# A gated linear attention with a maxout feed-forward block: the step list of the beginning in another order

## The chip, the cores and the metric

The kernel runs on one core of one Trainium2 chip. The metric is the device time of one execution in microseconds (us); a profile of one further execution shows the engines: TensorE (PE, matrix products), VectorE (DVE), ScalarE (ACT), GpSimd (POOL) and SyncE (SP, which here only issues transfers).

## The reference, cut to what matters

```python
# q, k, v, a_re, a_im: (4, 8, 768, 48); complex gates a, at most 0.999 in magnitude
a = a * min(|a|, 0.999) / (|a| + 1e-6)
for t in range(S):
    S_re, S_im = a_re*S_re - a_im*S_im + k[t] v[t]^T, a_re*S_im + a_im*S_re
    y[t] = q[t] @ S_re
x = y as (3072 tokens, 384)
h = max(x @ w1, x @ w2, x @ w3)        # w: (384, 768), float64 in memory
out = h @ w_out                        # (768, 384)
```

All inputs but the weights are float32. The recurrence is over 768 time steps for each of 4 x 8 heads.

## The kernel before, in words

**Tiles.** Time is cut into tiles of 128 steps, two halves of 64 each, for all 8 heads of one batch entry. Two batch entries, `x` and `y`, are worked side by side as a group; there are 12 groups (`NG`), six for each pair of entries. The recurrence inside a tile is turned into matrix products: the gates' logarithms and angles are summed along time, and queries and keys are scaled by exponentials and turned by sines before they are multiplied. The state is carried from tile to tile.

**Steps.** Every operation has a short name and a group number, such as `ukx:2` (step `uk`, batch entry x, group 2). `run` (line 747) maps a name to the function that issues its instructions. The names that matter here:

- `Lr`, `Li`, `Lq`, `Lk`, `Lv`: loads of the gates' real and imaginary part (one transfer of 192 KB), of q, k, v (four of 48 KB each), all from SP's queue.
- gates (line 372), on ACT and VectorE, for both entries at once or, in group 0, for one half (`0` or `1` at the end): `sqr`, `sqi`, `add`, `lnL`, `expe`, `expw`, `lne`, `relu`, `Lnop`, `abs`, `pw` (TensorE), `lnw`, `expL`, `mulw`, `mulai`, `stt`, `sign`, `cpai`, `cpar`, `atan`, `carry`, `mulr`, `addi`. Their results are a logarithm `Ln` and an angle.
- angles (452): `cs` sums the angle on TensorE, `t` and `nf` take off whole turns (ACT, VectorE), `af`, `sa`, `sb` make cosine and sine on ACT; `Cd` passes the last row to the next group by a transfer.
- turns (492): `sums`, `F` on TensorE sum the logarithm; `En`, `Ek`, `Eq`, `f0` to `f3` are exponentials on ACT; `mk`, `mq`, `uk`, `uq`, `kEn` scale and turn keys and queries on VectorE; `tpk`, `tpq` transpose them on TensorE; `Kc`, `Qc` copy them out on ACT.
- factors, scores, state, outputs (557 to 705): `Q1`, `Q2`, `Q3`, `QB`, `KB`, `QG` (VectorE); `A`, `B`, `dk`, `y` (TensorE); `g0` to `g3` and `h0` to `h3` (nearly all VectorE), `b0`, `b1` (ACT); `x` copies the tile's result, the feed-forward block's input, out of PSUM on ACT.
- up (712): `U` and two digits is an up product on TensorE (third of the hidden width, weight matrix), the same with a small `u` copies or takes the maximum (ACT for matrix 0, VectorE else). In group 0 there is one for each entry (`U20x`); later groups do both entries in one product of 256 columns. project (729): `O`, `o`, `D` are the down product, its copy and its store; in the list of the beginning `PO`, `Po`, `PD`.
- weights (301 to 346): they lie in memory as float64 and are turned into float32 on the chip, in twelve blocks: `WL` and a number is a block's load (768 KB), `Wa`, `Wd` are its steps on ACT, `Wb`, `Wc`, `We`, `Wf` on VectorE. A block's raw data lies in room that is later needed for something else, so a load can have to wait for the `Wf` of an earlier block.
- `Zf`, `Zv`, `Zg` clear buffers on VectorE; `CL` builds masks on GpSimd.

**What sets the order.** Nothing is left to a scheduler. `SCHEDULE` (line 21) lists the steps of the beginning, `CYCLE` (line 52) those of one group in the steady part, which `program` (787) runs for each group from 2 on. Each engine is wrapped in `Bound` (line 122), which makes every instruction follow the one before it on its engine, in the list's order; so SP, ACT, VectorE, TensorE and GpSimd are five queues, each in list order, that wait for one another only for data and buffers. All instructions are recorded through one line of that wrapper, 131, which is why the profile names this line throughout: steps are told apart by their tiles. TensorE's results go to four PSUM buffers in turn (`psum`, line 117): a product can start once the steps that read the fourth product before it are done. `activation` (150) loads another function table on ACT when the list goes from exponentials and logarithms to sines and arc tangents or back.

```python
def program(text, g):
    for word in text.split():
        name, at = word.split(":")
        run(name, g + int(at))
```

Of the kernel before, what the change touches and what calls it, by code (L numbers as in the profile page):

```python
# [56 lines left out]
cpai:1 g2x:0 QGx:0 cpar:1 Ox:-2 g3x:0 b0x:0 b1x:0 carry:1 mkx:1 KBy:0 U11:-1 mulr:1 addi:1 yx:0 xx:0 
u11:-1 kEny:0 ox:-2 U02:-1 csx:1 tx:1 csy:1 Q2y:0 ty:1 u02:-1 dky:0 sumsy:1 Lqx:1 nfx:1 sqi:2 mqx:1 afx:1
sbx:1 sax:1 nfy:1 h1y:0 Q1y:0 Eky:1 Q3y:0 Eny:1 h2y:0 Dy:-2 Fx:1 f0x:1 U12:-1 h3y:0 Eqy:1 uqx:1 u12:-1 Ay:0
add:2 f3x:1 g0y:0 g1y:0 By:0 g2y:0 f1x:1 f2x:1 lnL:2 g3y:0 QGy:0 expw:2 tpqx:1 expe:2 b0y:0 b1y:0 Oy:-1 ukx:1  # L60
relu:2 yy:0 tpkx:1 Qcx:1 xy:0
# [775 lines left out]
```

## Time and profile before

| | before |
|---|---|
| median of three runs | 626.19 us |
| the three runs | 624.35, 626.19, 628.63 us |
| the profiled execution's own time | 624.75 us |
| its span, first to last instruction | 622.9 us |
| TensorE, VectorE, ScalarE busy | 583.8, 478.9, 437.3 us |
| mean granted TensorE clock | 0.978 |

The span is cut into slices and stages below. Times of instructions are from the start of the span. "Busy" of TensorE is the time with a product under way, whether at full or at half clock; the granted clock is a share of full speed. A wait is idle time of an engine before an instruction, put down to the engine or transfer that ended it.

### The profile page before, as it was taken

What the parts mean: (1) busy time and instruction counts of PE and PEld (TensorE: products, weight loads), DVE (VectorE), ACT (ScalarE), POOL (GpSimd) and SP (SyncE); (2) the same over time, 40 slices, a digit from 0 to 9 for tenths busy, and PEclk for the clock granted to TensorE, in tenths of its full rate; (3) what the DMA queues carried; (4) which work ended last, traced back from release to release, by engine and by line L of the source; (5) the groups of instructions that cost most, each with busy time, mean ns of one, the idle gap of its engine ahead of it and who ended that gap; (6) DMA issues with size and microseconds to landing.
All of it is one profiled execution on the core that took longest, in us unless ns stands there. A gap on an engine that the chain in (4) does not pass through costs nothing.

```text
span 622.9 us, 22703 instructions
## 1 busy us (share of the span) xinstructions
PE 583.8 (94%) x10124; PEld 467.9 (75%) x10124; DVE 478.9 (77%) x694; ACT 437.3 (70%) x746; POOL 14.1 (2%) x47
## 2 busy tenths in 40 slices
PE   4376899999999999999999999999999999999997
PEld 1255787687887887887787788788788788788785
DVE  6998999989887887877777787887887887754211
ACT  8998998795894894894894994894894894641100
POOL 3500000000000000000000000000000000000000
PEclk9667999999999999999999999999999999999999
DMA  9787411442232223122222222222230221000000
GB/s 239 171 212 183 128 37 23 100 81 45 45 63 53 45 62 63 34 63 52 45 63 53 51 56 53 50 56 53 51 69 15 40 53 27 15 3 15 15 13 25
DMA packets 136544, 39.24 MB, mean 63 GB/s; under 512 B 129152, under 2 KB 132224, under 8 KB 136448
## 3 DMA queue, kind: packets, MB, share of 16 engines
q1 hardware_dynamic: 136448, 37.80, 27.5%
q8 instruction: 79, 1.29, 0.9%
q14 instruction: 17, 0.14, 0.1%
HBM read 33.03 MB, written 4.72 MB: 61 GB/s over the span
## 4 chain that ended last, share of the span: by engine, by line
PE 84%; ACT 7%; SPq 4%; DVE 3%; issue 1%; DMA 0%; DVEq 0%; ACTq 0%
PE up L131 44%; PE op L131 15%; PE y L131 6%; SPq L131 4%; PE A L131 4%; PE tp L131 4%; PE dk L131 3%; PE cs L131 2%; PE sums L131 2%; PE F L131 1%; ACT L131 1%; PE B L131 1%; DVE Q L131 1%; ACT L L131 1%; PE pw L131 1%
## 5 line engine op out<-in xcount | busy, mean ns | idle before, releaser
L131 PE MATMUL up<-xT,w 128*128 128x256 f32 (+1 forms) x1404 | 297.4, 368 | 2.4 <-ACT E L131 0.6
L131 PEld LDWEIGHTS up<-xT,w 128*128 128x128 f32 x1404 | 248.3, 191 | 40.1 <-ACT L L131 1.7
L131 DVE TENSOR_TENSOR hT<-hT,up 128x768 f32<-128x768 f32 (+1 forms) x56 | 46.8, 838 | 78.1 <-PE up L131 78.1
L131 PE MATMUL op<-wo,hT 128*128 128x384 f32 x288 | 98.8, 494 | 0.0
L131 DVE TENSOR_TENSOR Q<-Q,f 112x512 f32<-112x512 f32 (+2 forms) x72 | 68.6, 954 | 12.6 <-ACT Q L131 12.2
L131 PEld LDWEIGHTS op<-wo,hT 128*128 128x128 f32 x288 | 53.0, 190 | 33.4
L131 ACT ACT_TABLE_LOAD x47 | 60.3, 1283 | 1.6 <-PEq L821 0.8
L131 ACT COPY xT<-y 128x384 f32<-128x384 f32 x24 | 11.5, 479 | 51.6 <-PE y L131 51.6
L131 PE MATMUL y<-atm,vb 128*32 128x64 f32 x1152 | 39.4, 222 | 4.3 <-issue 3.0
L131 PEld LDWEIGHTS y<-atm,vb 128*32 128x32 f32 x1152 | 32.3, 110 | 14.2 <-issue 11.4
L131 ACT ACTIVATE f<-F 48x280 f32<-48x280 f32 x96 | 38.3, 399 | 2.5 <-PE F L131 1.2
L131 ACT ACTIVATE t<-cs 128x384 f32<-128x384 f32 x24 | 11.8, 492 | 39.0 <-PE cs L131 39.0
L131 PE MATMUL y<-QG,g 112*32 112x64 f32 x1408 | 38.4, 220 | 0.2 <-DVE QG L131 0.2
L131 ACT COPY atm<-B 32x128 f32<-32x128 f32 x96 | 24.4, 254 | 19.9 <-DVE atm L131 18.7
L131 PE MATMUL A<-Q,K 112*32 112x80 f32 x1536 | 32.9, 239 | 3.2 <-DVE Q L131 3.0
L131 PEld LDWEIGHTS y<-QG,g 112*32 112x32 f32 x1408 | 34.8, 110 | 0.5 <-DVE QG L131 0.3
L131 PEld LDWEIGHTS A<-Q,K 112*32 112x32 f32 x1536 | 28.1, 112 | 8.1 <-issue 3.1
L131 ACT COPY Q<-tp 112x1024 f32<-112x1024 f32 x24 | 24.3, 1013 | 12.2 <-PE tp L131 11.9
L131 DVE COPY_PREDICATED atm<-masko,A 128x256 f32<-128x256 uint8 x72 | 31.3, 435 | 1.4
L131 DVE TENSOR_TENSOR g<-g,dk 112x384 f32<-112x384 f32 x40 | 22.0, 550 | 9.7 <-PE dk L131 9.4
L131 PEld LDWEIGHTS dk<-vb,uk 64*48 64x48 f32 (+1 forms) x1408 | 23.5, 130 | 7.9 <-ACT K L131 2.7
L131 ACT COPY ot<-op 128x384 f32<-128x384 f32 x24 | 11.5, 478 | 25.5 <-PE op L131 25.4
(106 smaller groups left out, 887.9 us busy)
## 6 DMA issues: line engine op xcount, KB each, us to landing
ar<-in_a_re_dram SPq DMA_DIRECT2D x24, 192.0 KB
ai<-in_a_im_dram SPq DMA_DIRECT2D x24, 192.0 KB
q<-in_q_dram SPq DMA_DIRECT2D x96, 48.0 KB
k<-in_k_dram SPq DMA_DIRECT2D x96, 48.0 KB
vb<-in_v_dram SPq DMA_DIRECT2D x96, 48.0 KB
out_dram<-ot SPq DMA_DIRECT2D x24, 192.0 KB
raw<-in_moe_w_dram SPq DMA_DIRECT2D x5, 768.0 KB
w<-in_moe_w_dram SPq DMA_DIRECT2D x2, 768.0 KB
```

Source lines behind the costliest of these rows:

```text
L131: ins = f(*a, **kw)
```

## The change

Only the two lists at the top of the file differ. `CYCLE` holds the same steps in the same order and is only wrapped anew. `SCHEDULE` holds the same 467 steps in another order. GpSimd's instructions keep their order; on SP, ACT, VectorE and TensorE they are permuted. Among other moves: `Zg` stands ahead of `add0`; `sumsx:0` ahead of `pw0:0`; both key loads ahead of two weight blocks; `say:0` ahead of `b1x:0` and `b0x:0`; `tpky:0` ahead of `tpqy:0`, and both ahead of the first up product, which is now `U20x` and no longer `U00x`; `xx:0` behind `cpar:1`; the list ends on the same transposes. Cut to the stretches in question:

```diff
-Zf:0 Lrx:0 sqr0:0 Zv:0 Lix:0 sqi0:0 Liy:0 sqi1:0 add0:0 lnL0:0 expe0:0 expw0:0 Lry:0 sqr1:0 lne0:0 WL0:0
-relu0:0 Lnop0:0 Wa0:0 abs0:0 pw0:0 Wd0:0 add1:0 lnL1:0 Wb0:0 Wc0:0 We0:0 Wf0:0 WL1:0 Wa1:0 Wb1:0 Liy:1 Lry:1
-expe1:0 expw1:0 Zg:0 WL7:0 lne1:0 relu1:0 Lnop1:0 Lqy:0 Wd1:0 sumsx:0 lnw0:0 Wc1:0 We1:0 Wf1:0 abs1:0 Wa7:0
-Wb7:0 Wc7:0 pw1:0 Enx:0 Eqx:0 Lkx:0 expL0:0 mulw0:0 mulai0:0 stt0:0 lnw1:0 sign0:0 expL1:0 mulai1:0 mulw1:0
-Wd7:0 We7:0 Wf7:0 cpai0:0 Ekx:0 mkx:0 cpar0:0 CL:0 stt1:0 atan0:0 mulr0:0 csx:0 WL3:0 Wa3:0 Fx:0 Wb3:0 Wc3:0
-WL2:0 Lrx:1 Wa2:0 Wb2:0 Wc2:0 Wd2:0 We2:0 Wf2:0 sign1:0 sqr:1 Lix:1 Lqx:0 atan1:0 cpai1:0 Lky:0 tx:0 nfx:0
-cpar1:0 mulr1:0 Wd3:0 We3:0 Wf3:0 afx:0 Lvx:0 sbx:0 mqx:0 WL8:0 csy:0 Liy:2 sqi:1 Lry:2 WL6:0 Cdx:0 sax:0
-ukx:0 tpkx:0 uqx:0 tpqx:0 kEnx:0 f3x:0 add:1 f1x:0 f0x:0 f2x:0 ty:0 nfy:0 Qcx:0 Q1x:0 lnL:1 Q2x:0 dkx:0 WL4:0
...
-Wc6:0 abs:1 sumsy:0 Eny:0 g0x:0 Lky:1 We6:0 g1x:0 Fy:0 f3y:0 f2y:0 Eqy:0 mqy:0 f0y:0 Wa8:0 Wf6:0 g2x:0 Wb8:0
-Wd8:0 g3x:0 pw:1 lnw:1 Wc8:0 We8:0 Bx:0 f1y:0 Cdy:0 Eky:0 mky:0 WL5:0 Lrx:2 afy:0 WL9:0 expL:1 mulai:1 mulw:1
-stt:1 b1x:0 b0x:0 yx:0 sby:0 Lix:2 say:0 Lvy:1 uqy:0 tpqy:0 Lqx:1 uky:0 Lkx:1 sign:1 Wf8:0 WL10:0 xx:0 Lvx:2
-Lqy:1 U00x:0 cpai:1 carry:1 atan:1 cpar:1 mulr:1 tpky:0 kEny:0 Wa4:0 Wb4:0 Qcy:0 Q2y:0 QBy:0 Q1y:0 Wa5:0 Wb5:0
-csx:1 tx:1 nfx:1 Cdx:1 sqr:2 u00x:0 U01x:0 Kcy:0 KBy:0 Q3y:0 sqi:2 add:2 sbx:1 Wc4:0 u01x:0 afx:1 sax:1 Wc5:0
-sumsx:1 Ekx:1 Enx:1 csy:1 ty:1 Liy:3 Lix:3 Ay:0 g0y:0 QGy:0 Wd4:0 We4:0 Eqx:1 mqx:1 g1y:0 nfy:1 Cdy:1 lnL:2
-expe:2 expw:2 relu:2 lne:2 U02x:0 g2y:0 u02x:0 g3y:0 Wf4:0 Wa9:0 WL11:0 mkx:1 Lnop:2 Wb9:0 uqx:1 U10x:0 u10x:0
-U21x:0 Wd5:0 U20x:0 u20x:0 u21x:0 By:0 b0y:0 abs:2 We5:0 dky:0 h1y:0 Wc9:0 Fx:1 f3x:1 f1x:1 addw:2 h2y:0 Lvx:1
...
-f3y:1 Ax:1 g0x:1 f1y:1 kEnx:1 POx:0 Pox:0 Lrx:3 Lry:3 QBx:1 g1x:1 KBx:1 g2x:1 mqy:1 g3x:1 Bx:1 b0x:1 uqy:1
-Lqx:2 QGx:1 sqi:3 mky:1 h0x:1 uky:1 dkx:1 h1x:1 b1x:1 tpqy:1 Qcy:1 Q2y:1 h2x:1 POy:0 yx:1 sqr:3 add:3 Lkx:2
-Q1y:1 lnL:3 Poy:0 xx:1 h3x:1 tpky:1 Kcy:1 Fx:2 f1x:2 f0x:2 f3x:2 f2x:2 csy:2 ty:2 Q3y:1 Ay:1 h0y:1 sumsx:2
-Ekx:2 Enx:2 QBy:1 kEny:1 KBy:1 By:1 g0y:1 Eqx:2 nfy:2 sumsy:2 Eny:2 g1y:1 PDy:0 g2y:1 g3y:1 b0y:1 dky:1 b1y:1
-expe:3 mqx:2 uqx:2 tpqx:2 Qcx:2 expw:3 QGy:1 h1y:1 mkx:2 Eqy:2 Eky:2 yy:1 xy:1 relu:3 PDx:0 h2y:1 ukx:2 tpkx:2
-h3y:1
...
+Zf:0 Lix:0 Zv:0 Zg:0 sqi0:0 Lrx:0 sqr0:0 add0:0 Liy:0 sqi1:0 Lry:0 WL0:0 WL1:0 Lky:0 WL3:0 WL7:0 lnL0:0
+expe0:0 expw0:0 lne0:0 Lkx:0 relu0:0 Lnop0:0 sumsx:0 sqr1:0 add1:0 Wa0:0 Wb0:0 Wc0:0 abs0:0 pw0:0 lnL1:0 Wd0:0
+We0:0 Wf0:0 Wa1:0 Wb1:0 Wc1:0 expe1:0 expw1:0 lne1:0 relu1:0 Lnop1:0 Wd1:0 We1:0 Wf1:0 lnw0:0 abs1:0 Eqx:0
+Ekx:0 pw1:0 expL0:0 mulai0:0 mulw0:0 Enx:0 Wa7:0 stt0:0 mkx:0 sign0:0 Wb7:0 Wc7:0 WL2:0 Liy:1 Lix:1 Wd7:0
+We7:0 Wf7:0 cpai0:0 lnw1:0 cpar0:0 expL1:0 mulw1:0 Lqx:0 Lqy:0 mulai1:0 atan0:0 mulr0:0 csx:0 Wa3:0 Wb3:0
+Wa2:0 sign1:0 stt1:0 Lrx:1 Wd2:0 Lry:1 cpai1:0 Lvx:0 atan1:0 Wb2:0 Wc2:0 We2:0 tx:0 Fx:0 mqx:0 Wd3:0 nfx:0
+afx:0 sbx:0 Wc3:0 We3:0 CL:0 sax:0 ukx:0 tpkx:0 Wf3:0 WL8:0 WL4:0 uqx:0 tpqx:0 Wf2:0 WL6:0 f0x:0 cpar1:0
+mulr1:0 csy:0 f1x:0 kEnx:0 sqr:1 f3x:0 sqi:1 add:1 Qcx:0 f2x:0 QGx:0 Q1x:0 dkx:0 Q2x:0 Kcx:0 sumsy:0 KBx:0
...
+Wd8:0 afy:0 h3x:0 Wd6:0 Ax:0 g0x:0 Wc8:0 Eky:0 g1x:0 Fy:0 f2y:0 f0y:0 Wb6:0 f1y:0 pw:1 lnw:1 Eqy:0 f3y:0 g2x:0
+expL:1 Lqx:1 We8:0 Wf8:0 Wc6:0 mky:0 Eny:0 We6:0 Lix:2 Lrx:2 g3x:0 say:0 Liy:2 Bx:0 b1x:0 Lvy:0 Cdx:0 b0x:0
+yx:0 Wf6:0 Lvx:1 mulw:1 sby:0 sign:1 mulai:1 mqy:0 Wa4:0 stt:1 cpai:1 atan:1 WL5:0 uky:0 Lkx:1 Lky:1 tpky:0
+uqy:0 tpqy:0 Wb4:0 carry:1 Wc4:0 kEny:0 cpar:1 mulr:1 xx:0 U20x:0 Qcy:0 Q1y:0 QGy:0 Q2y:0 sqr:2 Kcy:0 Wa5:0
+Wb5:0 csx:1 tx:1 nfx:1 QBy:0 sqi:2 U21x:0 u20x:0 u21x:0 afx:1 Wd4:0 add:2 sax:1 Q3y:0 csy:1 ty:1 nfy:1 Cdy:1
+Wd5:0 U22x:0 u22x:0 Cdx:1 sbx:1 KBy:0 We4:0 lnL:2 Wc5:0 U00x:0 u00x:0 expe:2 WL9:0 expw:2 lne:2 relu:2 Wf4:0
+sumsx:1 Enx:1 Ekx:1 Eqx:1 Ay:0 U01x:0 dky:0 h1y:0 WL10:0 g0y:0 We5:0 g1y:0 u01x:0 By:0 g2y:0 Lnop:2 abs:2
+Lqy:1 g3y:0 b1y:0 b0y:0 U10x:0 mkx:1 Wa9:0 mqx:1 h2y:0 addw:2 lnw:2 u10x:0 uqx:1 h3y:0 Wb9:0 expL:2 yy:0 Lvy:2
...
+say:1 QBx:1 Ax:1 u02y:0 tx:2 g0x:1 POx:0 Lrx:3 Lry:3 nfx:2 afx:2 sbx:2 sax:2 g1x:1 KBx:1 Bx:1 g2x:1 kEnx:1
+dkx:1 Pox:0 g3x:1 b1x:1 b0x:1 Fx:2 uqy:1 tpqy:1 Qcy:1 sqi:3 h0x:1 mky:1 h1x:1 POy:0 QGx:1 h2x:1 f0x:2 f2x:2
+f1x:2 f3x:2 QBy:1 Lvy:1 h3x:1 yx:1 Q1y:1 Poy:0 PDy:0 Lqx:2 sqr:3 Q2y:1 uky:1 xx:1 tpky:1 Kcy:1 h0y:1 Q3y:1
+sumsx:2 Ekx:2 Enx:2 Eqx:2 PDx:0 csy:2 add:3 lnL:3 kEny:1 KBy:1 Ay:1 g0y:1 g1y:1 By:1 sumsy:2 ty:2 nfy:2 Eny:2
+g2y:1 QGy:1 g3y:1 dky:1 h1y:1 expe:3 b1y:1 mqx:2 b0y:1 expw:3 relu:3 mkx:2 Eqy:2 Eky:2 yy:1 xy:1 uqx:2 tpqx:2
```

More of the change, by code (lines that the diff above doesn't have):

```diff
@@ L27 @@
-WL2:0 Lrx:1 Wa2:0 Wb2:0 Wc2:0 Wd2:0 We2:0 Wf2:0 sign1:0 sqr:1 Lix:1 Lqx:0 atan1:0 cpai1:0 Lky:0 tx:0 nfx:0
-cpar1:0 mulr1:0 Wd3:0 We3:0 Wf3:0 afx:0 Lvx:0 sbx:0 mqx:0 WL8:0 csy:0 Liy:2 sqi:1 Lry:2 WL6:0 Cdx:0 sax:0
-ukx:0 tpkx:0 uqx:0 tpqx:0 kEnx:0 f3x:0 add:1 f1x:0 f0x:0 f2x:0 ty:0 nfy:0 Qcx:0 Q1x:0 lnL:1 Q2x:0 dkx:0 WL4:0
-Q3x:0 Kcx:0 Ax:0 QBx:0 expe:1 expw:1 Lvy:0 h1x:0 h2x:0 QGx:0 lne:1 KBx:0 relu:1 Lnop:1 Wa6:0 Wb6:0 Wd6:0 h3x:0
-Wc6:0 abs:1 sumsy:0 Eny:0 g0x:0 Lky:1 We6:0 g1x:0 Fy:0 f3y:0 f2y:0 Eqy:0 mqy:0 f0y:0 Wa8:0 Wf6:0 g2x:0 Wb8:0
@@ L37 @@
-expe:2 expw:2 relu:2 lne:2 U02x:0 g2y:0 u02x:0 g3y:0 Wf4:0 Wa9:0 WL11:0 mkx:1 Lnop:2 Wb9:0 uqx:1 U10x:0 u10x:0
-U21x:0 Wd5:0 U20x:0 u20x:0 u21x:0 By:0 b0y:0 abs:2 We5:0 dky:0 h1y:0 Wc9:0 Fx:1 f3x:1 f1x:1 addw:2 h2y:0 Lvx:1
-U22x:0 b1y:0 yy:0 u22x:0 f0x:1 h3y:0 tpqx:1 Wf5:0 lnw:2 expL:2 mulw:2 mulai:2 f2x:1 U11x:0 U12x:0 Wd9:0 We9:0
-stt:2 sign:2 xy:0 U20y:0 Qcx:1 u11x:0 Wf9:0 u12x:0 atan:2 ukx:1 cpai:2 Q2x:1 cpar:2 mulr:2 U10y:0 Wa11:0
-u20y:0 u10y:0 Lvy:2 carry:2 U21y:0 u21y:0 addi:2 U00y:0 Wa10:0 Q1x:1 u00y:0 Wb10:0 Wb11:0 U22y:0 Wc10:0 Wc11:0
@@ L42 @@
-u22y:0 sby:1 tpkx:1 U01y:0 Wd10:0 We10:0 U11y:0 u11y:0 u01y:0 Wd11:0 We11:0 U02y:0 u02y:0 afy:1 say:1 Wf11:0
-Q3x:1 Kcx:1 sumsy:1 Eny:1 Eky:1 Eqy:1 csx:2 tx:2 U12y:0 Fy:1 f0y:1 f2y:1 nfx:2 sbx:2 afx:2 sax:2 Wf10:0 u12y:0
-f3y:1 Ax:1 g0x:1 f1y:1 kEnx:1 POx:0 Pox:0 Lrx:3 Lry:3 QBx:1 g1x:1 KBx:1 g2x:1 mqy:1 g3x:1 Bx:1 b0x:1 uqy:1
-Lqx:2 QGx:1 sqi:3 mky:1 h0x:1 uky:1 dkx:1 h1x:1 b1x:1 tpqy:1 Qcy:1 Q2y:1 h2x:1 POy:0 yx:1 sqr:3 add:3 Lkx:2
-Q1y:1 lnL:3 Poy:0 xx:1 h3x:1 tpky:1 Kcy:1 Fx:2 f1x:2 f0x:2 f3x:2 f2x:2 csy:2 ty:2 Q3y:1 Ay:1 h0y:1 sumsx:2
@@ new lines @@
+Q3x:0 QBx:0 lnL:1 ty:0 nfy:0 Cdy:0 expw:1 expe:1 Lry:2 h1x:0 h2x:0 lne:1 relu:1 Lnop:1 Wa8:0 Wa6:0 Wb8:0 abs:1
+Wd8:0 afy:0 h3x:0 Wd6:0 Ax:0 g0x:0 Wc8:0 Eky:0 g1x:0 Fy:0 f2y:0 f0y:0 Wb6:0 f1y:0 pw:1 lnw:1 Eqy:0 f3y:0 g2x:0
+expL:1 Lqx:1 We8:0 Wf8:0 Wc6:0 mky:0 Eny:0 We6:0 Lix:2 Lrx:2 g3x:0 say:0 Liy:2 Bx:0 b1x:0 Lvy:0 Cdx:0 b0x:0
+yx:0 Wf6:0 Lvx:1 mulw:1 sby:0 sign:1 mulai:1 mqy:0 Wa4:0 stt:1 cpai:1 atan:1 WL5:0 uky:0 Lkx:1 Lky:1 tpky:0
+uqy:0 tpqy:0 Wb4:0 carry:1 Wc4:0 kEny:0 cpar:1 mulr:1 xx:0 U20x:0 Qcy:0 Q1y:0 QGy:0 Q2y:0 sqr:2 Kcy:0 Wa5:0
@@ new lines @@
+Wb5:0 csx:1 tx:1 nfx:1 QBy:0 sqi:2 U21x:0 u20x:0 u21x:0 afx:1 Wd4:0 add:2 sax:1 Q3y:0 csy:1 ty:1 nfy:1 Cdy:1
+Wd5:0 U22x:0 u22x:0 Cdx:1 sbx:1 KBy:0 We4:0 lnL:2 Wc5:0 U00x:0 u00x:0 expe:2 WL9:0 expw:2 lne:2 relu:2 Wf4:0
+sumsx:1 Enx:1 Ekx:1 Eqx:1 Ay:0 U01x:0 dky:0 h1y:0 WL10:0 g0y:0 We5:0 g1y:0 u01x:0 By:0 g2y:0 Lnop:2 abs:2
+Lqy:1 g3y:0 b1y:0 b0y:0 U10x:0 mkx:1 Wa9:0 mqx:1 h2y:0 addw:2 lnw:2 u10x:0 uqx:1 h3y:0 Wb9:0 expL:2 yy:0 Lvy:2
+xy:0 Wf5:0 Fx:1 f1x:1 sign:2 mulai:2 f0x:1 mulw:2 Lix:3 U11x:0 u11x:0 f3x:1 Wc9:0 f2x:1 stt:2 tpqx:1 Qcx:1
@@ new lines @@
+ukx:1 U02x:0 u02x:0 U12x:0 u12x:0 U20y:0 U00y:0 Q2x:1 Wd9:0 cpai:2 We9:0 atan:2 carry:2 cpar:2 mulr:2 WL11:0
+Wa11:0 u20y:0 Wf9:0 u00y:0 Q1x:1 Wa10:0 U21y:0 u21y:0 afy:1 Wb11:0 Wb10:0 U22y:0 u22y:0 tpkx:1 Kcx:1 Q3x:1
+Wd10:0 Wc11:0 U10y:0 U01y:0 u01y:0 Liy:3 U11y:0 Lvx:2 Wc10:0 sby:1 u10y:0 u11y:0 We10:0 addi:2 U12y:0 u12y:0
+Wd11:0 We11:0 Wf10:0 Fy:1 f0y:1 f2y:1 f1y:1 Wf11:0 f3y:1 sumsy:1 Eky:1 Eny:1 U02y:0 Lkx:2 csx:2 Eqy:1 mqy:1
+say:1 QBx:1 Ax:1 u02y:0 tx:2 g0x:1 POx:0 Lrx:3 Lry:3 nfx:2 afx:2 sbx:2 sax:2 g1x:1 KBx:1 Bx:1 g2x:1 kEnx:1
@@ L50 @@
+dkx:1 Pox:0 g3x:1 b1x:1 b0x:1 Fx:2 uqy:1 tpqy:1 Qcy:1 sqi:3 h0x:1 mky:1 h1x:1 POy:0 QGx:1 h2x:1 f0x:2 f2x:2
+f1x:2 f3x:2 QBy:1 Lvy:1 h3x:1 yx:1 Q1y:1 Poy:0 PDy:0 Lqx:2 sqr:3 Q2y:1 uky:1 xx:1 tpky:1 Kcy:1 h0y:1 Q3y:1
+sumsx:2 Ekx:2 Enx:2 Eqx:2 PDx:0 csy:2 add:3 lnL:3 kEny:1 KBy:1 Ay:1 g0y:1 g1y:1 By:1 sumsy:2 ty:2 nfy:2 Eny:2
+g2y:1 QGy:1 g3y:1 dky:1 h1y:1 expe:3 b1y:1 mqx:2 b0y:1 expw:3 relu:3 mkx:2 Eqy:2 Eky:2 yy:1 xy:1 uqx:2 tpqx:2
+Qcx:2 ukx:2 h2y:1 tpkx:2 h3y:1
 """
@@ L56 @@
 sign:1 tpqy:0 Qcy:0 tpky:0 u01:-1 QBx:0 Lkx:1 stt:1 Ax:0 Bx:0 h0y:0 Kcy:0 g0x:0 sqr:2 atan:1 g1x:0 QBy:0
[L57 to L61, printed above, removed]
+cpai:1 g2x:0 QGx:0 cpar:1 Ox:-2 g3x:0 b0x:0 b1x:0 carry:1 mkx:1 KBy:0 U11:-1 mulr:1 addi:1 yx:0 xx:0 u11:-1
+kEny:0 ox:-2 U02:-1 csx:1 tx:1 csy:1 Q2y:0 ty:1 u02:-1 dky:0 sumsy:1 Lqx:1 nfx:1 sqi:2 mqx:1 afx:1 sbx:1 sax:1
+nfy:1 h1y:0 Q1y:0 Eky:1 Q3y:0 Eny:1 h2y:0 Dy:-2 Fx:1 f0x:1 U12:-1 h3y:0 Eqy:1 uqx:1 u12:-1 Ay:0 add:2 f3x:1
+g0y:0 g1y:0 By:0 g2y:0 f1x:1 f2x:1 lnL:2 g3y:0 QGy:0 expw:2 tpqx:1 expe:2 b0y:0 b1y:0 Oy:-1 ukx:1 relu:2 yy:0
+tpkx:1 Qcx:1 xy:0
 """
```

## The prediction

> **What bounds the kernel now.** I read the page's slices first, then the stages, then who ended VectorE's idle time, then the clock, and last the end of the beginning in the chain.
>
> The page: busy tenths in 40 slices of 15.6 us, and the granted clock.
>
> ```profile
> span 622.9 us, 22703 instructions
> PE   4376899999999999999999999999999999999997
> DVE  6998999989887887877777787887887887754211
> ACT  8998998795894894894894994894894894641100
> PEclk9667999999999999999999999999999999999999
> ```
>
> TensorE is full from the sixth slice to the last; before that it is thin, and VectorE (DVE) and ScalarE (ACT) are the full ones. The stages (length, then busy us of each engine) say it in numbers:
>
> ```profile
> 9.50:62.00 52.50, 32.29 (x475) 22.00 (x474) 49.28 (x75) 49.63 (x83) 8.13 (x16) 0.74 0.81 199
> 62.00:82.00 20.00, 16.95 (x396) 14.77 (x392) 19.78 (x34) 19.32 (x34) 0.00 (x0) 1.00 0.46 122
> 82.00:126.20 44.20, 42.01 (x914) 34.21 (x910) 42.54 (x67) 37.90 (x67) 0.00 (x0) 1.00 0.25 51
> 126.20:580.00 453.80, 452.56 (x8090) 366.70 (x8088) 357.86 (x501) 319.15 (x539) 0.00 (x0) 1.00 0.23 47
> ```
>
> From 126.2 us on, TensorE works 452.6 of 453.8 us. The change doesn't touch that part, so only the moment at which it starts can move: 622.9 = 126.2 + 496.7. The chain, in order of time (start, length), shows what sets this moment:
>
> ```profile
> 120.53 0.56 DVE q L131
> 121.09 0.02 issue
> 121.12 0.96 DVE uq L131
> 122.07 1.15 DVE QG L131
> ...
> 125.63 0.66 PE tp L131 x16
> 126.29 7.97 PE up L131 x36
> ```
>
> It runs through VectorE until 123 us. The transpose at 125.63 is that of `ukx:2`, a VectorE product that ends at 125.48 in the timeline. From 9.5 us to there VectorE is busy 49.3 + 19.8 + 42.5 = 111.6 of 116.7 us. So the end of the beginning is VectorE's sum of work plus VectorE's own waits. Those are few:
>
> ```profile
> DVE Ln L131 <- ACT L L131: 3.1, 1, 3.1
> DVE uk L131 <- PE tp L131: 1.2, 1, 1.2
> DVE atm L131 <- PE A L131: 1.1, 2, 0.6
> ...
> DVE uq L131 <- ACT CS L131: 0.6, 1, 0.6
> DVE ai L131 <- ACT L L131: 0.4, 1, 0.4
> ```
>
> **The change part by part.** [...] VectorE's steps of the beginning sum to the same time, ACT switches its table set 8 times in either list (1.28 us each), and the last product needed, `ukx:2`, again closes VectorE's beginning. Hence the time moves only by VectorE's waits that go or come. I lay the new order of each engine end to end with the durations of its steps here, wait for what each step reads and for the PSUM buffer (four rotate), and compare at checkpoints.
>
> *The start.* `Zg` (four memsets, 1.09 us at 14.26) moves ahead of `add0`, into the time in which VectorE waits 3.13 us for ACT. Cover: that wait. But `add0` now ends near 7.5 us instead of 6.39 and ACT's chain behind it shifts: `lnL0`, `expe0`, `expw0`, `lne0`, `relu0` (0.43 each, `sqr1` now behind them) end at 9.85 against 9.48. `Wb0` starts at 11.1 (10.53 before), `We0` waits 0.5 for `Wd0`, which moved behind `lnL1`. Of 1.09 us some 0.2 is left at `Wf1` (18.1 against 18.31).
>
> *Loads.* The first four inputs and two weight blocks keep their place; `Lky`, `Lkx` (four DMAs each), `WL3` and `WL7` come next. SP needs about 2.5 us for four DMAs and packets land at some 240 KB per us (239 GB/s in the page's first slice). `Lkx` lands near 18.5 and is read at 19.8; `WL7` lands near 17, read at 18.6. Tight but covered. Later `WL8` waits on SP for `Wf3` (33 us) and `WL6` for `Wf2` (34.8); `WL4` and all other loads queue behind them. Three blocks of 768 KB at the 250 to 330 KB per us of the busiest slices land by 40.4 to 42.5; `Wa6` reads the last at 43.3. If they come late, `Wa6` stops ACT and all behind it by that much (next late: `expL:1`, then `mulw:1` on VectorE).
>
> *Three waits that go.* `mulai:1` waited 0.35 for `expL:1`: six VectorE steps now stand ahead of it, `expL:1` a little earlier. `uqy` waited 0.62 for `say`, which stood behind `b1x`, `b0x` and a table load: `say` now goes first. `kEny` waited 1.25 for `tpky`, which stood behind the first up product: `tpky` is now right behind `yx`, and the up product, now `U20x`, comes after both transposes. Sum 2.22, and with the start 2.4 us.
>
> *What takes their place.* `xx` moves behind `sby`, `sign:1`, `Wa4`, `cpai:1`, `atan:1`, `cpar:1` on ACT and ends at 59.1 instead of 56.4; TensorE idles from 58.1 to 59.1. Then `U20x`, then `csx:1`. `tx:1` (ACT) waits for `csx:1`, as it did before (1.19), with `sqr:2`'s successors queued behind it; `nfx:1` (VectorE) waits for `tx:1`, with `QBy`, `u21x`, `add:2`, `Q3y` behind. VectorE reaches `nfx:1` at 63.3. How long it waits depends on the clock. These are PE busy us and granted clock in four windows of 3.41 us:
>
> ```profile
> 15.95:19.37 3.42, 0.91 (x2) 1.00 0.60 100
> 33.02:36.43 3.41, 1.33 (x34) 1.00 1.00 289
> 50.09:53.50 3.41, 1.34 (x92) 1.00 1.12 326
> 56.91:60.33 3.42, 3.42 (x24) 0.50 0.32 59
> ```
>
> Behind each of the first three the clock is halved, though TensorE worked in all of them and its longest pause in the second was 1.8 us; behind the last, full one it stays at 1.00 to the end. So idle time summed over a window halves it and a full window restores it. The Trainium skill ("TensorE: Matmul & The Clock Gate", Part 1) has half rate after at least one idle window of about 3.4 us, and advises against single gaps over about 3 us. By that rule nothing after 45 us would halve the clock: `U20x` takes 1.36 at full clock (spacing of later up products), `csx:1` 1.5, `nfx:1` waits for nothing, and the whole 2.4 us stay. By the rows, the window from 56.9 holds the idle us, some 2.4 of 3.4 busy, and isn't full; the clock comes back only at 63.75. `U20x` then takes its 2.93, `csx:1` runs from 62.0 to 64.3, `tx:1` ends at 64.8 and `nfx:1` waits 1.5. I take the rows: 2.4 − 1.5 = 0.9 us left here. Bounds: 2.4, and −0.3 if `csx:1` runs wholly at half clock.
>
> *Later.* `g0x:1` waited 0.65 for `Ax:1`; `mqy:1`, `QBx`, `u02y` now cover it: −0.65. `h2y:1` (0.47) moves behind `ukx:2`, next to `tpkx:2`: −0.47. New small waits: ACT steps were moved nearer to their readers in some places (`mulai:2`, `nfy:2`, each within a few tenths); I allow +0.5. TensorE, 58 us of full-clock work from `U20x` on, would be through by about 119, so it has 4 to 5 us of cover; the moved up products cost nothing while that holds. `Lqx:2` now queues behind the output store `PDy` and lands near 119; `mqx:2` comes at 120.
>
> **Sum.** −0.9 − 0.65 − 0.47 + 0.5 = −1.5 us. Span 622.9 → 621.4; by the rule instead of the rows 619.9. The profiled execution's own time is 624.75 (1.85 around the span), so 623.2 on that footing; the median of the three runs, 626.19, lies 1.44 higher, and I carry the same 1.5 us over: **624.7 us**.
>
> **Rivals.**
> - *No effect: VectorE's sum rules.* For it: the same 111 us, the same last product, waits of only 5 us in all from 9.5 us on. Against: three of these waits visibly lose their cause. Time: 626.2, within 1 us.
> - *Loads come late.* For it: SP stands still from about 30 to 33 us behind `WL8`, while here `WL8` was issued at 31.33 and `WL6` at 33.69. Against: the DMA engines are idle in that pause and drain fast. If `Wa6` waits 2 to 4 us, the ACT chain passes 1.5 to 3.5 on: 626 to 629.
> - *Slower by over 1%: TensorE becomes the bound through the clock.* Each window at half clock takes 1.7 us of TensorE work. With a cover of 4.5 us it decides once the clock stays halved for three more windows after 63.75, to about 74 us; six windows cost 10 us, 10 − 4.5 − 1.5 = +4, eight +7.5, to 634. For it: the up products now start 2 us later and are spread singly between waits. Against: from 62 us on TensorE has 17 us of work in each 20 here, and one full window restores the clock.
> - *Faster by over 1%.* All of VectorE's 5 us of waits would have to go and 1.3 us of its small pauses too: below 620.
>
> **How the numbers follow.** Forecast (−0.5 to −4) 0.50: 622.2 to 625.7, its own range. No effect 0.20, loads late 0.12, slower clock 0.10, faster 0.08. About 1% (6.3 us) is what a measurement of this kernel can tell from no change. Faster than that 0.08 + a rest of 0.02; slower 0.10; the rest 0.80. The range must also take the runs' own scatter (624.35 to 628.63): 619.5 to 630.
>
> **What would show it.** Right: VectorE's rows lose the 1.2 (`uk` for `tp`) and the 0.6 (`uq` for `CS`), and a wait of `nf` for ACT `t` of about 1.5 near 64 appears; the clock is back for good in the window from 63.75; the long run of up products begins near 124.7. Wrong: a clock below 1.00 after 67 us, ACT waiting for a DMA near 43, or VectorE's waits between 9.5 and 126 us at 6 or more.

## The result and the profile after

| | before | after |
|---|---|---|
| median | 626.09 us (20 runs) | 624.59 us (20 runs) |
| range of the runs | 624.06 to 629.74 | 622.99 to 626.74 |
| profiled execution, own time | 624.75 us | 626.2 us |
| its span | 622.9 us | 624.3 us |
| ratio after to before | | 0.9972, 95% interval [0.996, 0.9984] |

The change brings 1.75 us of 626 (1.0 to 2.5). The two profiled executions show the opposite of the medians: that of before lies 1.34 us below its median, that of after 1.6 above. So the two traces can't be subtracted as wholes; each stretch has to be compared by itself.

The page of after, same rows as shown of before:

```profile
span 624.3 us, 22707 instructions
PE   3375999899999999999999999999999999999997
DVE  6999899979887887877777786887887887754211
ACT  7999897895894894894894993894894894641100
PEclk9675999999999999999999999999999999999999
```

The stages of after (length, then busy us of PE, its weight loads, DVE, ACT, POOL, granted clock, DMA share, GB/s):

```profile
9.50:62.00 52.50, 30.58 (x459) 22.00 (x460) 49.72 (x75) 51.57 (x87) 9.22 (x16) 0.69 0.71 177
62.00:82.00 20.00, 18.78 (x401) 16.18 (x401) 17.81 (x29) 18.14 (x34) 0.00 (x0) 0.96 0.35 104
82.00:126.20 44.20, 40.77 (x925) 34.02 (x921) 42.26 (x68) 37.59 (x67) 0.00 (x0) 1.00 0.38 81
126.20:580.00 453.80, 451.43 (x8083) 365.90 (x8084) 356.40 (x498) 318.93 (x538) 0.00 (x0) 1.00 0.23 47
```

VectorE is as full as before in the first stage and 2 us emptier in the second, where the clock is now 0.96 on the mean. TensorE lost 1.1 us in the last stage, which the change doesn't touch (the last section says by what). VectorE's waits of the beginning (us in all, times, longest):

```profile
DVE Ln L131 <- ACT L L131: 2.5, 1, 2.5
DVE nf L131 <- ACT t L131: 1.6, 1, 1.6
DVE Q L131 <- ACT Q L131: 1.2, 1, 1.2
...
DVE hT L131 <- PE up L131: 0.9, 2, 0.5
DVE atm L131 <- PE A L131: 0.7, 2, 0.5
...
DVE uk L131 <- ACT CS L131: 0.4, 1, 0.4
```

The rows `uk` for PE `tp` (1.2), `uq` for `CS` (0.6) and `ai` for `L` (0.4) are gone, and the wait of `nf` for `t`, 1.6, has come, as forecast. The row `uk` for `CS` (0.4) is new and was not forecast: where `uqy:0` waited for `say:0`, `uky:0` now waits for ACT. (The row `Q` is the wait of `Q1x:2` at 126.8, behind the beginning.) Where the new wait comes from, in the timeline of after (start, length, engine, operation, in brackets the idle time before):

```profile
59.54 2.93 PE L131 MATMUL up<-xT,w 128*128 128x128 f32 x12 [0.75 <-ACT xT L131]
62.40 0.92 PE L131 MATMUL cs<-ai,upto 128*64 128x192 f32 x4
...
64.56 0.49 ACT L131 ACTIVATE t<-cs 128x384 f32<-128x384 f32 x1 [1.71 <-PE cs L131]
...
65.08 0.55 DVE L131 SCALAR_TENSOR_TENSOR nf<-t,cs 128x384 f32<-128x384 f32 x1 [1.57 <-ACT t L131]
```

`U20x` takes 2.93 us at half clock, `csx:1` follows it, `tx:1` has waited for it 1.71 us and `nfx:1`, behind `tx:1`, 1.57 us. The times forecast for this stretch (`xx` done at 59.1, `csx:1` 62.0 to 64.3, `tx:1` done at 64.8) are met within 0.4 us: 59.5, 62.4 to 64.5, 65.05.

Now the end of the beginning. VectorE ends `ukx:2` at 124.57, 0.91 us earlier than before (125.48), but the long up products start at 126.12, only 0.10 earlier (126.22). The chain of after, in order of time:

```profile
122.84 0.87 DVE uq L131
123.70 0.87 DVE uk L131
124.57 0.48 DVE g L131
125.05 0.03 issue
125.08 1.12 PE tp L131 x32
```

The transposes start at 125.08 though `uqx:2` was ready at 123.70 and the product ahead of them, `yy:1`, done at 124.17. The chain names `g` (`h2y:1`), which is no operand of them. What TensorE waits for there is taken up below.

Where do the 0.91 us of VectorE come from? Its busy time from the start of the span to the end of `ukx:2`, in before, in this profile of after and in the two further ones (length, busy DVE with its count, granted clock, DMA share, GB/s):

```profile
0.00:125.48 125.48, 115.65 (x189) 0.89 0.56 136
0.00:124.57 124.57, 114.61 (x188) 0.86 0.54 135
0.00:122.42 122.42, 114.36 (x188) 0.90 0.58 138
0.00:122.95 122.95, 114.23 (x188) 0.88 0.57 136
```

What is left of the length is idle: 9.83 us in before, 9.96 in this profile, 8.06 and 8.72 in the others. So in the profiled execution VectorE doesn't wait less than before; it has 1.04 us less work ahead of `ukx:2`. Some 0.5 of that is `h2y:1`, which moved behind `ukx:2`; for the rest no cause is shown. In the other two executions 1.8 and 1.1 us of idle time go as well.

### The profile page after: what moved, and what is told of

It is laid out like the page before. It is cut to its first block, busy times and chain, and to the rows that moved or that the text cites. A ratio compares the mean times of both kernels' runs of the same rounds, so it can differ in the third digit from the quotient of the medians.

```text
span 624.3 us, 22707 instructions
## 1 busy us (share of the span) xinstructions
PE 581.8 (93%) x10124; PEld 468.6 (75%) x10124; DVE 478.0 (77%) x694; ACT 437.0 (70%) x746; POOL 15.1 (2%) x47
## 3 DMA queue, kind: packets, MB, share of 16 engines
q8 instruction: 79, 1.29, 0.9%
## 4 chain that ended last, share of the span: by engine, by line
PE 82%; ACT 7%; DVE 4%; DMA 3%; SPq 2%; issue 1%; DVEq 0%; ACTq 0%
PE up L131 43%; PE op L131 16%; PE y L131 6%; PE A L131 4%; PE tp L131 4%; PE dk L131 3%; PE cs L131 3%; PE sums L131 2%; SPq L131 2%; DMA w<-in_moe_w_dram 1%; PE F L131 1%; ACT L L131 1%; PE B L131 1%; DMA k<-in_k_dram 1%; ACT w L131 1%
## 5 line engine op out<-in xcount | busy, mean ns | idle before, releaser
L131 PE MATMUL A<-Q,K 112*32 112x80 f32 x1536 | 31.5, 234 | 0.7 <-ACT g L131 0.7
```

Source lines behind the costliest of these rows:

```text
L131: ins = f(*a, **kw)
```

## The experiments

Every kernel was timed beside the kernel before on one chip. Several were run again, so all times of the same kernel can be set beside one another: before 626.8 (mean of 130 runs in all, standard error 0.1), after 624.7 (44 runs, 0.2).

**After, unchanged**, for further traces.

> The changed kernel once more, for a second trace. Theory (VectorE's waits set the beginning): nf waits about 1.6 us for ACT t near 65, the clock is back for good near 63.6, and the first up product of group 1 starts near 126 us; time about 1.5 us below the kernel before. Rival (the gain lies in chance, such as where the clock's windows fall or a late instruction fetch): the checkpoints up to 126 us move by more than 1 us against the first trace.

624.8 us beside 626.72, ratio 0.9969 [0.9948, 0.999]; span 621.5 us. `nfx:1` doesn't wait here. The windows of the granted clock around it (length, busy PE, ...; the clock is the number behind POOL's), first in the first profile of after:

```profile
53.30:56.70 3.40, 2.18 (x80) 2.14 (x80) 3.00 (x5) 3.34 (x9) 0.00 (x0) 0.50 0.27 49
56.70:60.10 3.40, 2.65 (x42) 2.32 (x35) 3.31 (x6) 3.38 (x6) 0.00 (x0) 0.50 0.52 162
60.10:63.60 3.50, 3.50 (x20) 3.05 (x19) 3.41 (x5) 2.75 (x4) 0.00 (x0) 0.51 0.84 189
63.60:67.00 3.40, 3.40 (x36) 2.91 (x34) 1.92 (x4) 2.44 (x5) 0.00 (x0) 1.00 0.06 10
```

and of its second:

```profile
54.30:57.70 3.40, 3.40 (x102) 3.20 (x104) 2.93 (x5) 3.40 (x6) 0.00 (x0) 0.50 0.50 77
57.70:61.10 3.40, 2.32 (x32) 2.05 (x30) 3.40 (x6) 3.38 (x6) 0.00 (x0) 1.00 0.91 271
```

In the second execution the windows fall so that one, from 54.3 to 57.7, holds `yx:0` and `tpky:0` and is full; the clock is back at 57.7, `U20x` takes 1.6 us and `nfx:1` is 1.93 us earlier (63.71 against 65.64). In the first, two windows of 2.18 and 2.65 busy us follow each other and don't restore it; it is back at 63.6. So where the windows of 3.4 us happen to fall in an execution decides whether `nfx:1` waits 1.57 us or not at all. Of five traces with this stretch unchanged only the first has the wait. It isn't all in which executions differ: in the run with `g3y:1` first (below), whose list is the same up to here, `nfx:1` doesn't wait either and still starts at 65.06, as late as in the first trace of after (65.08), because VectorE got to `kEny:0` 1.35 us later (60.24 against 58.89). At the end of the beginning the second trace has `ukx:2` 2.15 us earlier than the first (122.42 against 124.57), and the up products 1.34 earlier (124.78 against 126.12).

**Before with one transpose moved**: `tpky:0` alone.

```diff
-... uky:0 Lkx:1 sign:1 ... U00x:0 cpai:1 carry:1 atan:1 cpar:1 mulr:1 tpky:0 kEny:0
+... uky:0 tpky:0 Lkx:1 sign:1 ... U00x:0 cpai:1 carry:1 atan:1 cpar:1 mulr:1 kEny:0
```

> The kernel before with one part of the change alone: the key transpose of entry y in front of the first up product. Theory (each VectorE wait that goes is time won): the wait of 1.25 us of uk for tp goes, everything on VectorE behind it comes 1.2 us earlier up to 126 us, time 1.2 us below the kernel before. Rival (ACT is as full as VectorE, so what VectorE wins is waited for at ACT again): VectorE waits in other places within 10 us, the last transpose of the beginning moves by less than 0.4 us, no change in time.

626.4 beside 626.72, ratio 1.0 [0.9982, 1.0019]. `kEny` and `nfx:1` are 1.6 us earlier, and 12 us on `Lnop:2` is 0.07 us earlier. The waits between 61 and 76 us in this run:

```profile
ACT t L131 <- PE cs L131: 1.7, 1, 1.7
...
DVE KB L131 <- ACT K L131: 1.0, 1, 1.0
DVE ex L131 <- ACT w L131: 0.6, 1, 0.6
```

`KBy:0` now waits 1.0 for `Kcy:0`, which stands on ACT behind `tx:1`, which itself waits 1.7 for `csx:1`. The wait that went has come back on the next step that needed ACT. A wait of VectorE that goes isn't by itself time won.

**Before with that transpose and its copy moved.** `Kcy:0` goes ahead of `tx:1` as well, as in the kernel after.

```diff
-... Q1y:0 Wa5:0 Wb5:0 csx:1 tx:1 nfx:1 Cdx:1 sqr:2 u00x:0 U01x:0 Kcy:0 KBy:0
+... Q1y:0 Kcy:0 Wa5:0 Wb5:0 csx:1 tx:1 nfx:1 Cdx:1 sqr:2 u00x:0 U01x:0 KBy:0
```

> The kernel before with tpky:0 ahead of the up product (as in the run with that move alone) and, on ACT, Kcy:0 ahead of Wa5:0 and tx:1 instead of behind u00x:0. The move alone put nfx:1 1.6 us earlier and lost it within 4 us: KBy:0 waited 1.0 for Kcy:0, which stood behind tx:1, which waited 1.7 for csx:1. Theory: ACT's order was the other half of the gain. Then Kcy:0 fits into ACT's wait for csx:1, KBy:0 doesn't wait, VectorE keeps 1.0 to 1.5 us (Lnop:2 at 74.5 to 75, ukx:2 at 124.0 to 124.5), and the time falls by 0.7 to 1.3 us: ratio 0.998 to 0.999. Rival: ACT's work as such (not its order) holds VectorE, so another wait for ACT of the same size comes within 10 us (Ln for e, or af, f), Lnop:2 stays at 75.9, ratio 1.0.

626.04 beside 626.85, ratio 0.999 [0.9972, 1.0009]. The trace kept the gain: `KBy:0` at 63.38 without a wait, `Lnop:2` at 73.92 (75.95 before), `ukx:2` at 123.69, the up products at 124.61. The time couldn't be told from no change, so it was run again:

> The kernel before with tpky:0 ahead of the up product and Kcy:0 ahead of tx:1, as once already: its trace showed ukx:2 1.8 us and the long up products 1.6 us earlier than before, its rounds a ratio of 0.999 with both no change and 0.997 inside the interval. Theory: the two moves carry most of what the whole new list wins; then ratio 0.997 to 0.9985 here, and the two runs together exclude 1.0. Rival: half of the 1.6 us belongs to that one execution (its clock came back at 59.3, 1 us earlier than in the trace of before), and the ratio is 0.999 to 1.0 again.

625.71 beside 627.09, ratio 0.9975 [0.9956, 0.9995]. Both runs together have a mean of 625.9 (24 runs, error 0.3) against 626.8: two moves of the 467 steps bring about 1.0 us (0.3 to 1.6) of the 2.1. Which of the other moves bring the rest, no run shows. This second trace has `ukx:2` at only 124.89 and the up products at 126.36, no earlier than before (126.22), with the clock back at 61.6 instead of 59.3: of 1.8 us at `ukx:2` in the one execution 0.6 are left in the other.

**After with `Zg` at its old place.**

```diff
-Zf:0 Lix:0 Zv:0 Zg:0 sqi0:0 ... expw1:0 lne1:0
+Zf:0 Lix:0 Zv:0 sqi0:0 ... expw1:0 Zg:0 lne1:0
```

> The kernel after with one part undone: Zg goes back from ahead of add0 to its old place behind expw1:0. The prediction's step: of Zg's 1.09 us only some 0.2 was left as gain at Wf1, because add0 and ACT's chain behind it shift; so Wf1 should end near 18.5 here, 0.2 to 0.3 later than in the kernel after (18.26), mkx:0 and all of VectorE behind it 0.2 to 0.3 us later, and the time 0.2 us above the kernel after, which these rounds can't tell from it. Rival: all of the 1.09 us was won by the move (mkx:0 came 4 us earlier for several moves together); then Wf1 ends at 19.3 and VectorE's end moves by 1.1 us, the time by 0.7 to 1.1.

625.28 beside 626.85, ratio 0.9967 [0.9948, 0.9986]. `Wf1` ends at 18.30; in the three traces of after 18.26, 18.14 and 18.33. The rival (1.1 us won) falls at this checkpoint; the time, 0.3 us above the kernel after on the mean, is too coarse to tell. The row of VectorE in this run:

```profile
8.87 0.56 DVE L131 SCALAR_TENSOR_TENSOR Ln<-L,e 128x384 f32<-128x384 f32 x1 [2.47 <-ACT L L131]
...
14.94 1.09 DVE L131 MEMSET g<- 128x256 f32 x4
```

VectorE waits 2.47 for ACT's `L` here and 2.5 in after: with `Zg` first, `add0` and ACT's chain shift by it, so the wait isn't filled, only pushed back by 1.1 us; what is saved at 14.9 us has been spent by then.

**After with the copy and the up product earlier still**: `xx:0` behind `Wa4:0`, `U20x:0` behind `tpqy:0`.

```diff
-mqy:0 Wa4:0 stt:1 cpai:1 atan:1 ... tpqy:0 Wb4:0 ... mulr:1 xx:0 U20x:0 Qcy:0
+mqy:0 Wa4:0 xx:0 stt:1 cpai:1 atan:1 ... tpqy:0 U20x:0 Wb4:0 ... mulr:1 Qcy:0
```

> The changed kernel with the copy of entry x's result moved up on ACT from behind cpar:1 to behind Wa4, and the first up product to right behind the two transposes. Theory (the late copy leaves TensorE idle, the window isn't full, the clock comes back a window late and nf waits 1.6 us): the up product starts near 58.9 instead of 59.5, the clock returns one window of 3.4 us earlier, near 60.2, nf waits less than 0.3 us, time 1 to 1.5 us below the changed kernel. Rival (VectorE's win is lost again to ACT or the loads): nf's wait goes, but the last transpose of the beginning stays within 0.4 us of 125.6.

625.62 beside 626.72, ratio 0.9983 [0.9963, 1.0002]. `U20x` starts at 58.62, `nfx:1` doesn't wait, but `carry:1` waits 0.8 for `cpai:1`, which is now later by `xx:0`; `ukx:2` ends at 123.14. No gain over the kernel after (mean 625.8 against 624.7); the wait of `carry:1` suggests that the place on ACT was one step too early.

**After with dummy products** that fill TensorE's idle time: ten identity products ahead of `pw:1`, thirteen ahead of `Bx:0`. They are extra work; nothing reads them.

```diff
-HOT = {}
+HOT = {("pw", 1): 10, ("Bx", 0): 13}
```

> The changed kernel with 23 further products of the identity by itself in TensorE's idle time near 48 to 54 us; their results are read by nobody. Theory (idle time summed over a window of 3.4 us sets the clock): the windows from 46 us on are full enough, the clock isn't halved at 50, the two transposes, the up product and the angle sums run at full rate (up 1.6 instead of 2.9, sums 1.6 instead of 2.1), nf waits less than 0.3 us; time up to 1.5 us below the changed kernel if ACT can follow. Rival (only a single pause of over 3 us halves it): the fillers shorten that pause as well, so the clock does the same; they differ in the window before 50 us, where the changed kernel has a pause of only 2.8 us.

627.33 beside 626.72, ratio 1.0009 [0.9993, 1.0026]. The windows of this run:

```profile
49.90:53.30 3.40, 2.60 (x51) 2.59 (x52) 2.68 (x5) 3.33 (x6) 0.00 (x0) 1.00 0.72 125
53.30:56.70 3.40, 2.23 (x89) 1.99 (x87) 2.62 (x4) 3.33 (x8) 0.00 (x0) 1.00 0.29 48
56.70:60.10 3.40, 1.51 (x48) 1.10 (x36) 3.33 (x6) 3.38 (x6) 0.00 (x0) 1.00 0.91 248
60.10:63.50 3.40, 3.06 (x14) 2.84 (x16) 3.40 (x5) 3.40 (x5) 0.00 (x0) 0.50 0.65 112
```

The clock stays full to 60.1 us, through windows of 2.60 and 2.23 busy us; behind one of 1.51 it is halved all the same, just where `csx:1` needs it (`nfx:1` waits 1.1), and ACT waits 1.2 for `pw:1` behind the dummies. At the end of the beginning the clock is halved once more, from 125.0 to 128.4, behind a window with 1.42 busy us, and the long up products start at 128.36, 3.1 us behind `ukx:2`. The time is 2.5 us above that of the kernel after: filling cost more than it protected, though this one trace can't divide the loss between the dummies' delay and the second halving.

**After with `csx:1` and `csy:1` ahead of the first up products.**

```diff
-mulr:1 xx:0 U20x:0 Qcy:0 ... sqi:2 U21x:0 u20x:0 u21x:0 afx:1 ... Q3y:0 csy:1 ty:1 nfy:1 Cdy:1 Wd5:0
+mulr:1 xx:0 Qcy:0 ... sqi:2 csy:1 U20x:0 afx:1 ... Q3y:0 U21x:0 ty:1 nfy:1 Cdy:1 u20x:0 u21x:0 Wd5:0
```

> The kernel after with csx:1 and csy:1 ahead of the first up products: U20x:0 moves from behind xx:0 to behind csy:1, U21x:0 behind Q3y:0, u20x:0 and u21x:0 behind nfy:1. The prediction's step: the 1.5 us that nfx:1 waits are U20x's 2.93 us at half clock ahead of csx:1. If that is so, csx:1 starts at 60.7 when mulr:1 is done, tx:1 ends at 62.9 to 63.4, and nfx:1 waits 0 to 0.3 instead of 1.57 in whichever window the clock comes back; VectorE is 1.3 us earlier at nfy:1, and 0.5 to 1.3 us remain at ukx:2, of which TensorE's fetch of its instructions lets through a part: time 0 to 0.8 us under the kernel after. Rival: the wait is only traded, because the up products come 3 us later and TensorE's four buffers then hold up csy:1, u21x:0 or U00x:0: nfx:1 no longer waits, but u21x:0, u22x:0 or u00x:0 wait as much, and the time is that of the kernel after or above.

625.99 beside 626.85, ratio 0.9987 [0.9968, 1.0006]. `nfx:1` starts without a wait, `nfy:1` ends at 67.60, 1.19 us earlier than in the first trace of after. Then (VectorE of this run):

```profile
68.92 0.42 DVE L131 TENSOR_TENSOR hT<-hT,up 128x256 f32<-128x256 f32 x1 [1.32 <-PE up L131]
70.19 0.42 DVE L131 TENSOR_TENSOR hT<-hT,up 128x256 f32<-128x256 f32 x1 [0.85 <-PE up L131]
```

`u21x:0` and `u22x:0` wait 1.32 and 0.85 for up products that come later now, `Lnop:2` ends at 77.12 (76.06 in after). The rival holds in this trace: the wait is traded. But the clock takes part: behind a window with 1.70 busy us it is halved again here from 62.2 to 65.6, in which the up products run, so the two waits aren't the order's alone. That `nfx:1` doesn't wait here proves little, since it didn't in most traces of after either; that `U20x` causes the wait where there is one rests on the timeline above.

**After with `g3y:1` ahead of `QGy:1`**, at the end of the beginning.

```diff
-g2y:1 QGy:1 g3y:1 dky:1
+g2y:1 g3y:1 QGy:1 dky:1
```

> The kernel after with one move at the end of the beginning: g3y:1 ahead of QGy:1 on VectorE (as in the kernel before). In the kernel after ACT waits 1.16 us before b1y:1 until g3y:1 is done, so the product yy:1 starts at 122.3, and then TensorE pauses 0.9 us (1.7 in its second trace) ahead of tpqx:2 with nothing left to wait for but its own instructions: a fetch of them begins at 122.7 in the one, 121.2 in the other, each time 1.0 to 2.4 us after yy:1's start, and TensorE resumes 2.3 to 2.5 us later. Theory: the fetch is set off by how far TensorE has read in its instructions, so an earlier yy:1 brings an earlier fetch. Then yy:1 starts 0.9 us earlier, the fetch too, and the long up products begin 0.9 us earlier after ukx:2 at unchanged time: ratio to before 0.995 to 0.996, some 0.8 us under the kernel after. Rival: the fetch comes at a time of its own; then yy:1 ends earlier, the pause grows by the same 0.9, and nothing is won.

624.27 beside 626.85, ratio 0.9968 [0.9951, 0.9984]. TensorE in this run:

```profile
121.25 0.32 PE L131 MATMUL y<-atm,vb 128*32 128x64 f32 x8 [0.43 <-ACT atm L131]
...
124.60 0.66 PE L131 MATMUL tp<-ident,uq 64*112 64x64 f32 x16 [1.15 <-DVE uq L131]
125.07 0.64 PE L131 MATMUL tp<-ident,uk 64*112 64x64 f32 x16
```

`yy:1` starts at 121.25 (122.32 in after). The next transfer of instructions to TensorE, 16 KB in the queue that the page calls "q8 instruction", starts at 121.9 (122.7), and the transposes start at 124.60 (125.08). The up products start 0.48 us earlier at the same `ukx:2` (124.62). The theory is half confirmed: the transfer starts 0.86 us earlier with TensorE, but less than half of the 1.07 us arrives at the up products, and nothing in the time: its mean of 624.6 (12 runs, error 0.4) is that of the kernel after, 624.7.

**Both: that move, and `xx:0` from behind `cpar:1` to behind `cpai:1`.**

```diff
-stt:1 cpai:1 atan:1 WL5:0 ... mulr:1 xx:0 U20x:0 Qcy:0
+stt:1 cpai:1 xx:0 atan:1 WL5:0 ... mulr:1 U20x:0 Qcy:0
-g2y:1 QGy:1 g3y:1 dky:1
+g2y:1 g3y:1 QGy:1 dky:1
```

> The kernel after with two moves: g3y:1 ahead of QGy:1 (as in the run with that move alone, which put yy:1 1.1 us and the long up products 0.5 us earlier), and xx:0 from behind cpar:1 to behind cpai:1 on ACT. There TensorE has just finished yx:0, and atan:1 and cpar:1 move back by 0.5 us only, with mulr:1 not due before that (one place earlier, ahead of cpai:1, carry:1 had to wait 0.8). Theory: U20x:0 then follows tpqy:0 without a pause, 0.7 us earlier, and the wait of nfx:1 falls by 0.7 where it is there (it is there only in executions whose clock comes back late); the two together give 0.5 to 1.2 us: 623.5 to 624.3, ratio to before 0.995 to 0.9965, the lowest of all. Rival: both gains end in TensorE's fetch of its instructions at 121 to 123 us, and the time is that of the kernel after beside it (0.9970).

> The kernel after, unchanged, beside the others: 624.6 to 625 and ratio 0.997 as in both runs of it so far. Its trace tells how often nfx:1 waits: where the clock is back before U20x ends (in 57.7 in one trace), no wait and 2 us less on VectorE; where it comes back at 63.6 (the other), 1.57. The kernel without either move of its rivals, for the comparison with them on one chip.

Side by side on one chip: 623.08 (6 runs) with both moves, 624.59 for the kernel after, 627.09 for before; ratios 0.9935 [0.9912, 0.9958] and 0.9959 [0.9944, 0.9975]. Six runs are few, so it was run again:

> The kernel after with g3y:1 ahead of QGy:1 and xx:0 behind cpai:1, once more, because its first rounds gave only six times. Theory: both moves hold in any execution (U20x:0 follows tpqy:0 without a pause; yy:1 starts 0.9 to 1.1 us earlier and TensorE's fetch of its instructions with it), so 623.0 to 624.0 and a ratio of 0.993 to 0.9955, and a trace with U20x:0 within 0.3 us of tpqy:0's end and the long up products 0.8 to 1.0 us behind ukx:2. Rival: the first six times were lucky; then 624.6 and 0.996 to 0.997 as for the kernel after.

624.17 beside 627.17, ratio 0.9955 [0.994, 0.997]. TensorE in this last run:

```profile
58.16 1.06 PE L131 MATMUL tp<-ident,uq 64*112 64x64 f32 x16
59.15 1.05 PE L131 MATMUL up<-xT,w 128*128 128x128 f32 x7
```

`U20x` follows the transpose without the pause of 0.75 us, and the up products start at 123.88 in both traces (126.12, 124.78 and 124.50 in those of after). All 18 runs have a mean of 623.9 (error 0.25) against 624.7 (0.2) of the kernel after: 0.8 us better, 0.2 to 1.4. It is the best of the versions, though part of the comparison goes across chips. `xx:0` at its new place was not run alone, so the gain isn't divided between the two moves.

## Why the prediction was right, point by point

The time came out, 624.7 forecast and 624.59 measured, and so did the waits that were named: three go, one comes. The path from there to the time did not: in the profiled execution VectorE's waits bring nothing in sum, and a gain of VectorE doesn't reach the up products whole.

- **The moment at which the up products start is set by VectorE's work and waits: half right.** The chain still runs through VectorE to `uk` and from there to the transposes. VectorE's gain at `ukx:2` is 0.91, 3.06 and 2.53 us in the three traces of after. But the forecast carried such a gain one to one to the up products, and there it is 0.10, 1.44 and 1.72. This is the step that failed: TensorE was taken to be free at the end, with 4 to 5 us of cover. It isn't; see the last section. And the work ahead of `ukx:2` isn't the same: it is 1.0 to 1.4 us shorter, where the forecast had only `h2y:1`'s 0.47.
- **`Zg` (0.2 of 1.09 left): right.** Undoing it moved `Wf1` by less than 0.2 us.
- **Loads (tight but covered): right, with nothing to spare.** In the profile of after neither VectorE nor ACT waits for one of the loads that were named, nor ACT for any near 43 us. In the third trace of after and in the run with `g3y:1` first, `mkx:0` waits 0.2 and 0.4 us for `Lkx`. ACT waits 0.7 us near 90 for a load of the output weights. The rival of late loads, 2 to 4 us, falls. One transfer was overlooked: `Lqy:2` in the first group of the cycle was issued 3.7 us later than before and VectorE waited 1.8 for it until 134.4; TensorE hardly noticed: it worked 22.53 of the 23.8 us up to 150 (22.66 before).
- **Three waits go (2.22): right in what goes**, all three rows; in place of one of them `uky:0` waits 0.4 us (0.8 in the third trace). And the run with one transpose alone shows that such a row isn't a gain by itself: of that 1.6, 1.0 was waited for again at `KBy:0`, and only with ACT's new order beside it (`Kcy:0` ahead of `tx:1`) is about 1 us of time kept. The forecast had listed what the transposes free and not what ACT had to do for it.
- **In their place, `nfx:1` waits 1.5 for `U20x` at half clock: right for the profiled execution** (1.57; clock back at 63.6, forecast 63.75) **and oversized for the median**. The forecast laid the windows of before's trace over the new list. That they lay within 0.2 us of that in the profiled execution was luck: the windows lie elsewhere in each execution, and four of five traces had the clock back by 60.1 and no wait. The rows against the rule of the Trainium skill ("TensorE: Matmul & The Clock Gate", Part 1: half rate after one idle window of about 3.4 us): the rows hold against that rule. Windows with 0.91, 1.33, 1.34 and 1.51 busy us halved the clock, none of them idle; those with 2.23 to 2.60 kept it; at half clock one with 2.65 didn't restore it and ones with 3.06 and 3.40 did. But the busy time of a window draws no sharp border: 1.78 us halved the clock in the third trace of after (14.1 to 17.5), and 1.74 kept it in the first (43.1 to 46.5).
- **Later (−0.65, −0.47, +0.5):** not settled piece by piece. With the `nf` wait VectorE's gain was 0.91, where the terms sum to 1.5. Of new small waits 0.5 was allowed; `hT`, waiting 0.9 for up products, and `uk` with 0.4 alone are above that.
- **TensorE bound by the clock (rival): no.** The clock is 1.00 from 63.6 us to the end. **No effect, faster by over 1% (rivals): no**, the interval of 0.996 to 0.9984 excludes both.
- **Its signs.** Two rows went, the `nf` wait came and the clock was back at 63.6, as it said for right. The up products began at 126.12 there and not near 124.7 (124.78 and 124.50 in the other traces of after). And one of its signs for wrong came true: between 9.5 and 126.2 us VectorE is idle 6.9 us (109.8 of 116.7 busy; in before 5.1), above the 6 it named.

So in the two executions of after without the `nf` wait VectorE is 2.5 and 3.1 us earlier than in the one trace of before, more than forecast, and TensorE gives back 0.8 to 1.6 us that weren't forecast. That the sum of both lies near 1.5 is partly luck.

What stays open: before's profiled execution was fast for it (span 622.9, 2 us below what its mean time allows), so where its usual executions are slower is seen only in part. One us of it can be the pause near 371 us (last section), which nine of fourteen traces have and this one has not; the rest may lie in the clock's windows, but no trace shows it.

## What to carry to other kernels

When one engine's waits go, ask at once who released the next step on it: of 1.6 us taken off VectorE, nothing was seen in the time until ACT's queue was put in order too. Then follow the gain to the engine that sets the end, and look there for time in which it waits for nothing named. Count the engine's idle time as well as its rows: the waits that were named went, and the idle time of the profiled execution stayed. And one trace is one draw: take two or three before a stretch of 2 us is read as an effect of the edit.
